# Decays of the first three blocks and their q and k, prepared on the chip instead of through DRAM and DMA transpositions

## The chip, the cores and the metric

The kernel runs on one core of one Trainium2 chip. The metric is the device time of one execution in microseconds, from the runtime's measurement around it. The engines are PE (TensorE, matmuls; its weight loads are PEld), DVE (VectorE), ACT (ScalarE), POOL (GpSimd) and SP (SyncE, which here only issues DMAs).

## The reference

Three stages follow each other over 4 batches (B) of 768 time steps (S). The first is a gated recurrence with 8 heads of 40, with a running maximum m that keeps the exponentials small:

```python
for t in range(S):
    m_new = np.maximum(f_gate[:, :, t] + m, i_gate[:, :, t])
    f_stab = np.exp(f_gate[:, :, t] + m - m_new)
    i_stab = np.exp(i_gate[:, :, t] - m_new)
    m = m_new
    C = f_stab[:, :, None, None] * C + i_stab[:, :, None, None] * np.einsum('bhd,bhe->bhde', vt, kt)
    n = f_stab[:, :, None] * n + i_stab[:, :, None] * kt
    h_tilde = np.einsum('bhde,bhe->bhd', C, qt)
    ...
    y[:, :, t] = o * h_tilde / np.maximum(np.abs(nq), 1.0)
```

The second is a gated MLP: relu(x @ w_in) is cut into u and v, v is normalised and mixed over time by w_spatial (768 x 768), and u times that goes through w_out. The third picks two of four experts for each step, and each expert is causal softmax attention with one head of 64. All inputs and the output are float32.

## The kernel before

**Tiling.** Time is cut into blocks of 128 steps, six to a batch, so there are 24 blocks n = (b, c). The recurrence is done a block at a time: inside a block as a matrix of decays times q-k products, between blocks through a state `cs`. Units of up to three blocks then go through the MLP, whose spatial mix needs whole batches, and through the attention. Float32 operands are mostly used as pairs of float16, a high part (a cast) and a low part (a subtraction), and a product is then three float16 matmuls. For the first NF = 6 blocks the product with v is done in float32 instead (vo,dd).

**The order.** The work is written as threads (generators) that yield the engine they want next and the buffers or signals they need. `ORDER` is a table of some thousands of thread names; `Flow.run` walks it and lets the named thread record its next piece. So the table alone sets in which order each engine's queue is filled. It was made by a planner that prices instructions with `_cost` (line 48), with DMAs and DMA transpositions among them. The strings of `CFG` say for each cast or subtraction which engine does it (a is ACT, v DVE, p POOL), and `on(what, x)` reads them. All instructions are recorded in one helper, so nearly all carry line L154, and the trace is read by the names of tiles.

**The head of the program.** `gates(j)` (line 576) loads the gates of half of the batches (j = 0: batches 0 and 1) into the tile aT, makes running sums (ff) and maxima (mm) by scans, and with two small matmuls carries the maxima over blocks. It then cuts the row of exponents into three bfloat16 parts, and `send` (648) writes each part with two DMAs to r_dram in DRAM. `ones` (654) fills the constant part of r_dram and clears the tile rows. `columns` (669) turns two gate rows into columns g_c and w_c. `m_load` (868) loads q and k (qkf), then v and the output gate (vo), and with a third DMA fetches six rows per head back from r_dram into rows. In `m_decay` (888) eight bfloat16 matmuls of these rows per block (four per PSUM bank g) give the exponents of the decay matrix, ACT takes the exponential of 128 x 512 at a time into dd, and POOL clears the part above the diagonal (affine_select). `mlstm` (1005) casts q and k into qs and transposes it with one DMA transposition per block (qkT<-qs, line 1028, issued on SP). `weights` multiplies q by k on PE, and DVE multiplies the product by dd (`dd<-g,dd`, called the first and second product of a block here). Then come the product with v (pn; vo,dd in float32), the part from the state (cs,qkT; none in a batch's first block), num, den, the output gate, a cast xs and its DMA transposition x1T<-xs, which feeds the MLP's first matmuls (wi,x1T).

**The loads of weights.** Beside this the weights w_in, w_spatial, wqkv, w_out come in through DMAs issued on ACT's queue. Float64 words are turned into float32 on DVE with three bit instructions (`u<-vn` and two `u<-vn,u`), then split into two float16 parts. They are most of what DVE does in the first 60 us besides the recurrence.

## Time and profile before

| | value |
|---|---|
| median of 3 runs | 523.35 us (520.78, 523.42, 523.35) |
| the profiled execution | 523.3 us, its span 521.6 us |
| PE busy in the span | 467.3 us (90%) |
| DVE | 435.6 us (84%) |
| ACT | 325.4 us (62%) |
| POOL | 272.2 us (52%) |
| granted TensorE clock, mean | 0.999 |

The span runs from the first instruction to the last; 1.7 us of the time lie around it. A busy share is a mean over a program whose head, middle and tail differ, so a table of stretches says more. Which of TensorE's two rates (1.2 or 2.4 GHz) holds is read from the duration of equal matmuls at two places. The float32 matmuls show as two records each: 16 records of vo,dd are eight matmuls.

### The profile page before, as it was taken

The page shows a single profiled execution, that of the slowest core. Times are in us where ns is not written, and L with a number is a line of the kernel's source. Part 1 is how long each engine was busy: PE and PEld are TensorE (multiplying, and loading weights), DVE is VectorE, ACT ScalarE, POOL GpSimd, SP SyncE. Part 2 cuts the span into 40 slices and gives each one's busy share as a digit, 9 for nine tenths or more (in the row PEclk, how much of TensorE's full clock was granted, in tenths as well). Part 3 has the DMA queues.
Part 4 walks back from the last instruction along what each step waited for, and adds up shares of the span by engine and source line. Part 5 has one row for each costly group of instructions (what it writes and reads, how often), then busy time and mean ns, then how long its engine had stood idle before and what let it go on. Part 6 is the DMA issues. An engine that isn't in the chain of part 4 may idle for free.

```text
span 521.6 us, 14133 instructions
## 1 busy us (share of the span) xinstructions
PE 467.3 (90%) x5288; PEld 336.5 (65%) x5288; DVE 435.6 (84%) x1133; ACT 325.4 (62%) x796; POOL 272.2 (52%) x437
## 2 busy tenths in 40 slices
...
GB/s 227 196 206 218 206 160 135 152 95 110 104 109 117 170 168 183 181 155 200 206 163 128 124 205 162 161 136 156 120 152 100 168 117 110 126 150 143 185 83 39
DMA packets 180443, 78.58 MB, mean 151 GB/s; under 512 B 160342, under 2 KB 169880, under 8 KB 180376
## 3 DMA queue, kind: packets, MB, share of 16 engines
...
## 4 chain that ended last, share of the span: by engine, by line
PE 54%; DVE 14%; DMA 13%; issue 6%; POOL 5%; ACT 4%; SPq 2%; ACTq 0%; POOLq 0%; DVEq 0%
PE g L154 51%; PE pst L154 3%; DMA x1T<-xs 3%; SPq L154 2%; DMA aT<-ahl 2%; POOL ahl L154 2%; DMA r_dram<-aT 2%; DMA rows<-r_dram 2%; DVE qs L154 2%; DMA qkst<-qkh 1%; DVE dd L154 1%; DVE vo L154 1%; ACT ee L154 1%; DVE u L154 1%; ACT aT L154 1%
## 5 line engine op out<-in xcount | busy, mean ns | idle before, releaser
L154 PE MATMUL g<-wsT,vn 128*128 128x384 f16 (+2 forms) x612 | 94.5, 307 | 0.0
L154 PEld LDWEIGHTS <-vn 128*128 128x128 f16 x648 | 59.3, 98 | 30.6
L154 POOL TENSOR_TENSOR ahl<-ee,ahl 128x128 f16<-128x128 f32 (+5 forms) x51 | 49.8, 981 | 29.4 <-DVE ahl L154 17.1
L154 POOL TENSOR_SCALAR_AFFINE_SELECT dd<-dd 128x512 f32<-128x512 f32 x48 | 36.4, 765 | 51.0 <-ACT dd L154 50.8
L154 PE MATMUL g<-wi,x1T 128*128 128x512 f16 x192 | 48.9, 400 | 4.8 <-DMA x1T<-xs 2.2
L154 ACT ACTIVATE ee<-g,sm 128x128 f32<-128x128 f32 (+3 forms) x64 | 33.4, 523 | 27.3 <-DVE sm L154 19.7
L154 PE MATMUL g<-gT,w_h 128*128 128x384 f16 (+2 forms) x288 | 47.6, 308 | 0.0
L154 PE MATMUL g<-x1T,wi 128*128 128x384 f16 (+2 forms) x288 | 46.4, 308 | 1.0 <-ACT u L154 0.5
L154 PEld LDWEIGHTS <-qkst 128*128 128x128 f16 x424 | 34.7, 98 | 18.2 <-issue 4.9
L154 DVE SCALAR_TENSOR_TENSOR dd<-g,dd 128x512 f32<-128x512 f32 x48 | 32.2, 680 | 13.8 <-PE g L154 8.3
L154 ACT ACTIVATE ee<-pst,sm 128x640 f32<-128x640 f32 (+1 forms) x32 | 27.1, 847 | 25.6 <-DVE sm L154 14.4
L154 ACT ACTIVATE vn<-vn,nt 128x512 bf16<-128x512 f32 (+1 forms) x48 | 36.3, 761 | 4.9 <-POOL nt L154 4.5
L154 DVE CUSTOM_DVE_ANT_0 g<-g,mask 128x128 f32<-128x128 f32 (+3 forms) x64 | 30.9, 502 | 7.7 <-PE g L154 7.6
L154 ACT ACTIVATE dd<-g 128x512 f32<-128x512 f32 x48 | 27.6, 593 | 15.5 <-PE g L154 15.3
L154 PE MATMUL g<-qkst 128*128 128x384 f16 (+4 forms) x224 | 34.9, 290 | 2.5 <-issue 2.3
L154 PEld LDWEIGHTS <-wi 128*128 128x128 f16 x288 | 26.2, 97 | 16.0 <-issue 2.8
L154 DVE CUSTOM_DVE_ANT_0 pst<-pst,mask 128x640 f32<-128x640 f32 (+1 forms) x32 | 28.5, 895 | 9.5 <-PE pst L154 9.0
L154 DVE TENSOR_TENSOR ahl<-ee,ahl 128x768 f16<-128x768 f32 (+5 forms) x45 | 33.5, 749 | 2.5 <-ACT ahl L154 1.8
L154 PEld LDWEIGHTS <-x1T 128*128 128x128 f16 x192 | 18.2, 100 | 26.1 <-issue 3.9
L154 PEld LDWEIGHTS <-w_h 128*128 128x128 f16 x288 | 26.4, 98 | 13.2
L154 PE MATMUL g<-vv,aT 128*128 128x64 f16 x1008 | 34.4, 193 | 0.4 <-ACT aT L154 0.4
L154 PEld LDWEIGHTS <-aT 128*128 128x128 f16 x1008 | 32.6, 98 | 1.9 <-ACT aT L154 0.5
...
## 6 DMA issues: line engine op xcount, KB each, us to landing
...
```

Of the source, the lines that this page charges most:

```text
L154: r = f(*args, **kw)
```

## The change

For the first three blocks (n < NE = 3) the decays come from a float32 copy f_e of the row ff: one float32 matmul per head spreads one row of f_e over 128 partitions, with a broadcast column of the identity as its stationary operand. The other half of the exponent is a column of i_c, which a new thread `first` makes with one PE transposition; it enters as the bias of the exponential, so that there are eight exponentials of 128 x 128 for a block instead of two of 128 x 512. These blocks fetch no rows from r_dram. For the same three blocks (n < NQ = 3) q and k are transposed by 16 PE transpositions into PSUM and two copies to qkT (thread `flip`), instead of the DMA transposition; qkf is given free after the copies. The planner's prices are raised for DMAs (250 in place of 290 bytes/ns) and DMA transpositions (210 in place of 180 ns per 128 columns). The whole table ORDER and all strings of CFG are new; two of them are shown.

```diff
@@ -50,11 +50,11 @@
-        return 1300.0 + 225.0 * max(0.0, n - 8.0), 1090.0 - 26.0 * n, (900.0, 180.0 * n + 40.0), False
+        return 1300.0 + 225.0 * max(0.0, n - 8.0), 1090.0 - 26.0 * n, (900.0, 210.0 * n + 40.0), False
-        return 335.0 if lane == "act" else 740.0 if across else 550.0, 1500.0 + o.nbytes() / 600.0, (600.0, 40.0 + max(60.0, o.nbytes() / 290.0)), False
+        return 335.0 if lane == "act" else 740.0 if across else 550.0, 1500.0 + o.nbytes() / 600.0, (600.0, 40.0 + max(60.0, o.nbytes() / 250.0)), False
@@ -319,175 +319,179 @@
...
 CFG = dict(
+    qt="aaaaaa",
+    fe="a",
+    ic="a",
...
-    Wl="------------vvvvvvvvvpvvvpvvpvvvvvvvvvvvvvvvvvpv",
...
-    vnl="ppvvvvvppvvvpvvvvpvpvvvv",
...
+    Wl="------------vvvvvvvvpvvvpvvpppvpvvvpvpvppvpvvpvv",
...
+    vnl="pppvvvpvvpvppvpvppvvpppv",
...
-TIM = dict(NF=6, NP=2, NX=21, last=(0, 1, 2, 3, 4, 5), units=((3, 3), (3, 3), (3, 3), (3, 2, 1)))
+TIM = dict(NQ=3, NE=3, NF=6, NP=2, NX=21, last=(0, 1, 2, 3, 4, 5), units=((3, 3), (3, 3), (3, 3), (3, 2, 1)))
 ORDER = """
-PX2 PX1 PO0 PW0 PW2 PO1 PW1 PO2 PG1 PO1 PG0 PL0 PX3 PI0 PG1 PW0 PX3 PG1 PS1 PG0 PG1 PG0 PG1 PL0 PO1 PG0 PM0 FS0 PG0
+PX2 PX1 PO1 PO0 PW2 PW1 PO2 PW0 PG1 PS1 PL0 PG0 PX3 PS4 PO1 PG1 PG1 PW1 PG1 PL0 PD0 PM0 PG1 FS0 PM0 PX3 PS1 PG1 FS1
...
@@ -562,6 +566,8 @@
     g_c = cp.tile([P, B, H, NC], F32, name="g_c")
     w_c = cp.tile([P, B, H, NC], F32, name="w_c")
     f_b = cp.tile([P, B, H, NC], F32, name="f_b")
+    f_e = cp.tile([96, P], F32, name="f_e")
+    i_c = cp.tile([P, 96], F32, name="i_c")
     r_dram = dr.tile([6, B, H, NC, 2, P], BF16, name="r_dram")
     wi = cp.tile([P, 2, 3, 1024], F16, name="wi")
     wi_h, wi_l = wi[:, 0], wi[:, 1]
@@ -593,6 +599,8 @@
         dve.tensor_tensor_scan(ff, ft, zt[:R], 0.0, op0=ALU.add, op1=ALU.add)
         dve.tensor_tensor(it, it, ff, op=ALU.subtract)
         dve.tensor_tensor_scan(mm, it, it, NEG, op0=ALU.max, op1=ALU.max)
+        if j == 0:
+            flow.fork(first(it), "FI", 0)
         mp, re = (row[0:1, x, 0:96].rearrange("p (g c) -> p g c", c=NC) for x in (3, 4))
         rfc = row[0:1, 5, 0:96]
         yield pe, "g"
@@ -616,13 +624,17 @@
         dve.tensor_copy(mc[:, 0:1], pc[:R, 128:129])
         dve.tensor_scalar(mc[:, 1:2], mm[:, P - 1:P], mc[:, 0:1], -1.0, op0=ALU.max, op1=ALU.mult)
         dve.tensor_scalar(ff, mm, mc[:, 0:1], None, op0=ALU.max)
+        if j == 0:
+            yield on("fe", 0)
+            on("fe", 0).cast(f_e, ff)
+            flow.signal("fe", 0)
         yield act
         act.activation(ft, ff, AF.Exp, bias=mc[:, 0:1], scale=-1.0)
         act.activation(mm, it, AF.Exp, bias=mc[:, 1:2])
         flow.signal("gw", j)
         flow.fork(columns(j, ft, mm), "FT", j)
         for x in range(3):
-            yield on("pc", 3 * j + x), *[("a", j, x - 2)] * (x > 1)
+            yield on("pc", 3 * j + x), *[("a", j, x - 2)] * (x > 1), *[("ic", 0)] * (j == 0 and x == 0)
             p = pcs[:, 2 * (x % 2):2 * (x % 2) + 2]
             on("pc", 3 * j + x).cast(p, am)
             flow.signal("pcs", j, x)
@@ -645,6 +657,17 @@
         yield dve, ("gc", 2 * j), *[("a", j, x) for x in range(3)]
         flow.done("aT", "aT")
 
+    def first(it):
+        R = 96
+        yield pe, "g"
+        pt = bank(R)
+        pe.transpose(pt, it, ident[:R, :R])
+        flow.signal("ip", 0)
+        yield on("ic", 0)
+        on("ic", 0).cast(i_c, pt)
+        flow.done("g")
+        flow.signal("ic", 0)
+
     def send(j, x, p):
         yield sp, ("pcs", j, x), ("rd", 0)
         for y in range(2):
@@ -878,7 +901,9 @@
         m["vf"], m["ex"] = (vo[:, x:y].rearrange("p (h d) -> p h d", h=H) for x, y in ((0, 328), (328, 648)))
         sp.dma_start(vo, qkvo[b, c, :, 640:1288])
         flow.signal("vo", n)
-        yield sp, "rw", seq("rw", n), ("rz", 0), *[("a", b // 2, x) for x in range(3)]
+        if n < TIM["NE"]:
+            return
+        yield sp, "rw", seq("rw", n - TIM["NE"]), ("rz", 0), *[("a", b // 2, x) for x in range(3)]
         m["own_rw"] = flow.take("rw")
         sp.dma_start(rows[0:6].rearrange("k h x s -> k h (x s)"), r_dram[:, b, :, c].rearrange("k h x s -> k h (x s)"))
         flow.signal("rw", n)
@@ -887,19 +912,29 @@
 
     def m_decay(n):
         b, c = divmod(n, NC)
-        yield pe, "dd", ("rw", n), seq("dd", n)
+        yield pe, "dd", ("qk" if n < TIM["NE"] else "rw", n), seq("dd", n)
         m = ml[n]
         m["dd"], m["own_dd"] = tile_("dd", [P, H, P]), flow.take("dd")
         dd = m["dd"]
 
         def half(g):
-            yield pe, "g", seq("de", 2 * n + g)
+            yield pe, "g", *[("fe", 0)] * (n < TIM["NE"]), seq("de", 2 * n + g)
             src = bank()
             for h in range(4):
-                pe.matmul(src[:, h * P:h * P + P], rows[:, 4 * g + h, 0], rows[:, 4 * g + h, 1], start=True, stop=True)
+                k = (4 * g + h) * NC + c
+                if n < TIM["NE"]:
+                    pe.matmul(src[:, h * P:h * P + P], ident[:96, k:k + 1].to_broadcast([96, P]), f_e, start=True, stop=True)
+                else:
+                    pe.matmul(src[:, h * P:h * P + P], rows[:, 4 * g + h, 0], rows[:, 4 * g + h, 1], start=True, stop=True)
             flow.signal("de", n, g)
-            yield act
-            act.activation(dd[:, 4 * g:4 * g + 4].rearrange("p h t -> p (h t)"), src, AF.Exp)
+            if n < TIM["NE"]:
+                yield act, ("ic", 0)
+                for h in range(4):
+                    k = (4 * g + h) * NC + c
+                    act.activation(dd[:, 4 * g + h], src[:, h * P:h * P + P], AF.Exp, bias=i_c[:, k:k + 1], scale=-1.0)
+            else:
+                yield act
+                act.activation(dd[:, 4 * g:4 * g + 4].rearrange("p h t -> p (h t)"), src, AF.Exp)
             flow.done("g")
             yield pool
             pool.affine_select(dd[:, 4 * g:4 * g + 4], dd[:, 4 * g:4 * g + 4], pattern=[[0, 4], [1, P]],
@@ -908,8 +943,9 @@
 
         for g in range(2):
             flow.fork(half(g), "FH", 2 * n + g)
-        yield pe, ("de", n, 0), ("de", n, 1)
-        flow.done(m["own_rw"])
+        if n >= TIM["NE"]:
+            yield pe, ("de", n, 0), ("de", n, 1)
+            flow.done(m["own_rw"])
 
     def m_out(n):
         yield act, ("vo", n)
@@ -1022,10 +1058,29 @@
 
         flow.fork(stack(1), "FS", 2 * n + 1)
         flow.fork(stack(0), "FS", 2 * n)
-        yield sp, "qkT", ("qs", n, 0), ("qs", n, 1), seq("qkT", n)
-        flow.done(m["own"])
-        qkT = tile_("qkT", [P, 16, P], F16)
-        sp.dma_start_transpose(out=qkT, in_=qs.rearrange("p a d -> p (a d)"))
+        if n < TIM["NQ"]:
+            yield pe, "qkT", seq("qkT", n)
+            qkT = tile_("qkT", [P, 16, P], F16)
+
+            def flip(x):
+                yield pe, "g", ("qs", n, x)
+                pt = bank().bitcast(F16).rearrange("p (k t) -> p k t", k=8)
+                for h in range(8):
+                    pe.transpose(pt[:120, h], qs[:, 8 - 8 * x + h, :120], ident_h)
+                yield on("qt", 2 * n + x)
+                on("qt", 2 * n + x).cast(qkT[:120, 8 - 8 * x:16 - 8 * x], pt[:120])
+                flow.done("g")
+                flow.signal("qt", n, x)
+
+            flow.fork(flip(1), "FX", 2 * n + 1)
+            flow.fork(flip(0), "FX", 2 * n)
+            yield pe, ("qt", n, 0), ("qt", n, 1)
+            flow.done(m["own"])
+        else:
+            yield sp, "qkT", ("qs", n, 0), ("qs", n, 1), seq("qkT", n)
+            flow.done(m["own"])
+            qkT = tile_("qkT", [P, 16, P], F16)
+            sp.dma_start_transpose(out=qkT, in_=qs.rearrange("p a d -> p (a d)"))
         flow.signal("qT", n)
         flow.fork(m_state(n), "FM", n)
         Ws = [None, None]
```

SP's queue at the start, before. rows and r_dram are the gate rows, qkf, vo the inputs of a block, qs and qkT its q and k:

```order
L154 DMA aT<-in_f_gate_dram 96x128 x2
L154 DMA qkf<-in_qkvo_dram 128x640
L154 DMA r_dram<-rows 576x1x128 x2
L154 DMA vo<-in_qkvo_dram 128x648
L154 DMA_TRANSPOSE qkT<-qs 128x16x128
L154 DMA r_dram<-aT 96x128 x2
L154 DMA qkf<-in_qkvo_dram 128x640
L154 DMA r_dram<-aT 96x128 x4
L154 DMA vo<-in_qkvo_dram 128x648
L154 DMA rows<-r_dram 6x8x256 x2
L154 DMA_TRANSPOSE qkT<-qs 128x16x128
```

And now:

```order
L154 DMA aT<-in_f_gate_dram 96x128
L154 DMA qkf<-in_qkvo_dram 128x640
L154 DMA aT<-in_f_gate_dram 96x128
L154 DMA vo<-in_qkvo_dram 128x648
L154 DMA r_dram<-rows 576x1x128 x2
L154 DMA qkf<-in_qkvo_dram 128x640
L154 DMA r_dram<-aT 96x128 x2
L154 DMA vo<-in_qkvo_dram 128x648
L154 DMA r_dram<-aT 96x128 x2
L154 DMA qkf<-in_qkvo_dram 128x640
L154 DMA qkst<-ee 64x256 x4
L154 DMA r_dram<-aT 96x128 x2
```

The transposition of block 0 stood before the sends of the gate rows; now the loads of three blocks and the sends come first, and the first rows<-r_dram and qkT<-qs stand some ten rows further down.

PE's queue at the start, before (the small matmuls on aT belong to the gates):

```order
L154 MATMUL g<-ident,aT 1x96 x4
L154 MATMUL g<-ones_83,aT 96x1 x2
L154 MATMUL g<-ident,aT 128x96 x4
L154 MATMUL g<-aT,ones_83 128x96
L154 LDWEIGHTS rows
L154 MATMUL g<-rows 128x128
```

And now, where ident_h,qs are the transpositions and f_e,ident the new decays:

```order
L154 MATMUL g<-ident,aT 1x96 x2
L154 MATMUL g<-ones_83,aT 96x1
L154 LDWEIGHTS qs
L154 MATMUL g<-ident_h,qs 120x128
...
L154 MATMUL g<-ones_83,aT 96x1
L154 MATMUL g<-ident,aT 128x96
L154 MATMUL g<-f_e,ident 128x128 x8
L154 MATMUL g<-ident,aT 128x96 x2
L154 MATMUL g<-f_e,ident 128x128 x4
```

Block 0's 16 transpositions stand between the small matmuls of the two halves of the gates, and its eight decays directly behind the second half's first ones, where the queue went on to the columns and then to the rows of r_dram.

DVE's queue around the first products, before (rows 46 to 53):

```order
L154 SCALAR_TENSOR_TENSOR qs<-qkf,qs 128x8x40
L154 TENSOR_SCALAR ee<-u 128x256
L154 SCALAR_TENSOR_TENSOR qkst<-vn,qkst 128x512
L154 COPY f_b<-g 128x96
L154 SCALAR_TENSOR_TENSOR dd<-g,dd 128x512 x2
L154 TENSOR_SCALAR u<-vn 128x256
L154 SCALAR_TENSOR_TENSOR u<-vn,u 128x256 x2
L154 SCALAR_TENSOR_TENSOR ee<-u,ee 128x256
```

And now (rows 50 to 58):

```order
L154 SCALAR_TENSOR_TENSOR qs<-qkf,qs 128x8x40
L154 SCALAR_TENSOR_TENSOR wi<-u,wi 128x256
L154 SCALAR_TENSOR_TENSOR ee<-u,ee 128x256
L154 SCALAR_TENSOR_TENSOR dd<-g,dd 128x512
L154 TENSOR_SCALAR u<-vn 128x256
L154 SCALAR_TENSOR_TENSOR u<-vn,u 128x256 x2
L154 SCALAR_TENSOR_TENSOR dd<-g,dd 128x512
```

The first product stands three rows further down the queue than before, and the two products of block 0 have a weight's three bit instructions between them.

## Rows read from the trace of the kernel before

**Rows 1.** Stretches of the span: length, then busy us (instructions) of each engine
```profile
core 0: us, PE busy (x) PEld busy (x) DVE busy (x) ACT busy (x) POOL busy (x), PEclk, DMA share, GB/s
0.00:35.00 35.00, 8.09 (x65) 5.88 (x66) 22.51 (x65) 13.23 (x36) 11.41 (x28) 1.00 0.81 200
35.00:65.00 30.00, 20.93 (x166) 16.74 (x164) 27.66 (x68) 15.83 (x38) 12.05 (x20) 1.00 0.89 223
65.00:105.00 40.00, 37.07 (x330) 24.45 (x329) 35.35 (x78) 28.73 (x66) 20.36 (x34) 1.00 0.66 146
105.00:521.60 416.60, 401.21 (x4733) 289.44 (x4730) 350.11 (x925) 267.58 (x658) 228.34 (x357) 1.00 0.72 142
```

**Rows 2.** Waits of PE, 0 to 70 us: us in total, times, longest
```profile
PE g L154 <- ACT aT L154: 11.7, 3, 9.0
PE g L154 <- DMA rows<-r_dram: 11.1, 3, 5.4
PE g L154 <- DVE aT L154: 7.8, 3, 4.1
```

**Rows 3.** Chain of waits, 0 to 60 us: start us, us, what
```profile
14.98 6.35 DMA r_dram<-aT
...
27.16 3.51 DMA rows<-r_dram
30.80 2.29 PE g L154 x36
...
44.31 3.16 SPq L154
...
58.38 5.93 DMA x1T<-xs
```

**Rows 4.** Timeline of DVE: start us, us, instruction, [idle before, what ended it]
```profile
20.23 0.29 DVE L154 TENSOR_SCALAR u<-vn 128x256 uint32<-128x256 uint32 x1 [2.33 <-DMA vn<-in_w_in_dram]
...
33.19 1.29 DVE L154 SCALAR_TENSOR_TENSOR dd<-g,dd 128x512 f32<-128x512 f32 x2 [4.93 <-PE g L154]
...
63.40 0.50 DVE L154 TENSOR_TENSOR num<-g,g_c 128x328 f32<-128x328 f32 x1 [1.76 <-PE g L154]
```

**Rows 5.** Tile qkT up to 75 us: SP's transpositions, min/median/max ns, first and last start
```profile
L154 SPq DMA_TRANSPOSE qkT<-qs x5: 1658/2177/3158, 11.2 to 65.4; - x5
```

**Rows 6.** The stretch up to the second product of block 6, columns as in Rows 1
```profile
0.00:104.60 104.60, 65.69 (x555) 46.88 (x556) 85.11 (x209) 57.43 (x138) 43.51 (x80) 1.00 0.77 187
```

**Rows 7.** Timeline of PE: start us, us of the group, instruction and records
```profile
24.66 0.74 PE L154 MATMUL g<-aT,ones 1*128 1x96 f32 x2 [8.99 <-ACT aT L154]
...
32.48 1.02 PE L154 MATMUL g<-qkT 120*128 120x128 f16 x8
...
35.12 3.58 PE L154 MATMUL g<-vo,dd 128*128 128x41 f32 x16
...
64.35 3.59 PE L154 MATMUL g<-wi,x1T 128*128 128x512 f16 x8 [0.99 <-DMA x1T<-xs]
...
85.07 1.88 PE L154 MATMUL g<-vo,dd 128*128 128x41 f32 x16
```

**Rows 8.** Groups by line and form, whole span: busy us, mean ns, idle before
```profile
L154 ACT ACTIVATE dd<-g 128x512 f32<-128x512 f32 x48 | 27.6, 593 | 15.5 <-PE g L154 15.3
L154 ACT ACTIVATE ee<-g,sm 128x128 f32<-128x128 f32 x16 | 5.8, 363 | 8.6 <-DVE sm L154 7.3 <-POOL ahl L154 1.0
L154 DVE TENSOR_TENSOR Wl<-dd,Wh 128x512 f16<-128x512 f32 x32 | 22.3, 700 | 1.1 <-POOL Wh L154 0.5 <-ACT Wh L154 0.5
L154 POOL TENSOR_TENSOR Wl<-dd,Wh 128x512 f16<-128x512 f32 x4 | 6.9, 1735 | 0.7 <-ACT Wh L154 0.7
L154 DVE TENSOR_TENSOR vn<-vn 128x512 f16<-128x512 f32 x17 | 12.6, 743 | 0.6 <-POOL vn L154 0.6
L154 POOL TENSOR_TENSOR vn<-vn 128x512 f16<-128x512 f32 x7 | 8.9, 1275 | 4.4 <-DVE vn L154 4.3
```

**Rows 9.** Waits of PE over the whole span, columns as in Rows 2
```profile
PE g L154 <- DMA x1T<-xs: 2.2, 4, 1.0
...
PE g L154 <- DMA oT<-os: 1.4, 1, 1.4
```

319 lines of the change are left out of this document (160 added, 159 removed).

## The prediction

> **What bounds the kernel now.** I read the table of stretches first, because a mean over 521.6 us hides where an engine is idle. PE is idle for 26.9 us of the first 35, for 9.1 of the next 30, for 2.9 of the next 40, and for 15.4 of the 416.6 that remain [rows 1]. From 105 us on PE works 96% of the time and is the bound there. Before 65 us it is starved, and the change is made there: whatever brings the head of the program to its end earlier is gained, if the rest keeps its shape.
>
> Then the waits of PE up to 70 us: 11.7 us for ACT on the gate tile aT, 11.1 for the DMA rows<-r_dram, 7.8 for DVE on aT [rows 2]. The chain of waits says which of them count. Its head goes through the DMAs that send the gate rows to DRAM, the DMA that fetches them, 2.29 us of PE and then DVE; later through a transposition's 3.16 us on SP and a fetch of x1T [rows 3]. This is the path that the change cuts.
>
> The third reading is DVE, which must not be left out: it is idle in only 19.5 of the first 104.6 us [rows 6], and between 33 and 62 us its timeline has no gap. From the first product on, DVE sets the pace of the head, with PE behind it. Its two waits that matter are 4.93 us for PE's first q-k product at 28 to 33 us, and 2.33 us for a load of w_in at 18 to 20 us [rows 4]. So the gain is bounded by what DVE gets back, not by PE's 26.9 us of idle time.
>
> **The parts, on DVE's clock.** I sum up to the second product of block 6 (dd, DVE; it ends at 104.6 us before), behind which both orders have the same pipeline.
>
> The first product. Before, it needs rows fetched from DRAM. After, block 0 needs only f_e and the transposed q and k, which PE makes itself. The cast of f_e stands behind the second gate scan, at about 14 us. Then come 8 f32 matmuls, 8 exps, and the mask on POOL. A price for the matmul with 128 columns in f32 is not in the trace. The nearest row is the f32 vo,dd at the low clock, 16 records that are 8 matmuls in 3.58 us, or 0.448 each. The low end is the same at the high clock, 1.88/8 = 0.235. The high end is 2 records (one f32 matmul of 96 columns) in 0.74 [rows 7]. I take 0.448, since PE is at the low clock here: 3.6 us for the eight. An exp of 128 columns takes 0.363 [rows 8], 8 of them 2.9 us. With the mask the inputs of the first product are there by about 23 us. In the new order DVE has about as much work ahead of its first product as before, row 53 against row 50, and reaches it at 33.2 - 4.9 - 2.3 = 26 us. So both waits can go: the whole 4.9, and 2.3 for the w_in load, which ran beside the first transposition (its issue starts at 11.2 and holds SP for some 3 us [rows 5]) that is now gone. Bounds: 4.9 goes unless f_e costs the high end (then 8 x 0.74 is 2.3 later, still in time); the 2.3 may stay whole. **-7.2 us** (bounds -4.9 and -7.2).
>
> What DVE takes on. At that second product of block 6 the new order has passed 201 rows of DVE against 190, with ten more instructions ahead (casts that ACT and POOL did, a relu, two vn subtractions). By the stretch's mean, 85.11/209 = 0.407 us [rows 6], ten cost 4.1; by the shorter forms that most of them have, some 3.0. **+3.0** (to +4.1). It is not work that can hide: DVE has no gaps there.
>
> PE's new work. It gets 24 f32 matmuls (24 x 0.448 = 10.8), 48 transpositions of 120 x 128 at the price of qkT x8, 1.02/8 = 0.128 [rows 7] (6.1), and loses 24 rows matmuls at about the same 0.128 (3.1): +13.8 us at the low clock. The 36.0 us of PE idle before 65 us cover it in sum, but not in place. Blocks 1 and 2 put 16 f32 matmuls (7.2 us) and 16 transpositions (2.0) between DVE's products, less 2.0 of rows matmuls. DVE then waits for the numerator of block 1 or 2. The nearest row is its wait of 1.76 us for num at 63.40 [rows 4]. A new wait of 0 to 4 us is possible, the upper end if half of the 7.2 us falls where DVE stands; I take **+1.0**, nearer that row than the end.
>
> ACT's new work is 24 exps for 6 (24 x 0.363 - 6 x 0.593 = 5.1 us) and six copies of 1024 columns, at most two exps of 512 columns each, so 7.1 us. ACT is idle for 21.8 us before 35 and for 14.2 before 65 [rows 1], so this is put at nothing. If ACT is late instead, the masked decay comes late, and that wait is already the +1.0.
>
> SP. Three transpositions leave the queue, of 1.66 to 3.16 us each [rows 5], and three fetches of rows. The sends of the gate rows (from 14.98 on) and x1T come forward. The sends no longer feed block 0, only block 3. The 3.16 us of SP and the fetch behind it in the chain [rows 3] are then not on DVE's path for block 2. But DVE had no wait there, so I count nothing more for it.
>
> Three spatial matmuls fewer stand ahead of the point on PE: **+0.5**. The longer stretch after it: DMA waits of PE, 2.2 for x1T and 1.4 for oT [rows 9]. The new plan prices DMAs higher and so starts them earlier; I take **-1.0** (0 to -3.6). PE's order elsewhere keeps its shape, so its other idle time is kept.
>
> Sum: -7.2 + 3.0 + 1.0 + 0.5 - 1.0 = -3.7. Against the profiled execution, 523.3 us (521.6 of span and 1.7 around it), that is **519.6 us**. The median of the three runs is 523.35, so no correction is needed; one of the three was 520.78.
>
> **The rivals.**
>
> A larger gain, 515.5 us. PE has dense f32 work from about 14 us on instead of gaps. Its clock could rise before 35 us, and not at 69 as now: the vo,dd matmuls take 3.58 us for 16 at 35 us and 1.88 at 85, and the first 512-column matmuls at 64 us still go at the low rate [rows 7]. At the high rate the new work costs 13.8 x 1.88/3.58 = 7.2 and the +1.0 vanishes. The old 20.93 us of PE work between 35 and 65 [rows 1] would shrink by up to 20.93 x (1 - 1.88/3.58) = 9.9, of which I let 3.1 reach the end, as DVE's work doesn't shrink: 519.6 - 1.0 - 3.1 = 515.5. Against it: the new matmuls still come in groups between waits. The Trainium skill, "TensorE: Matmul & The Clock Gate", section "Part 4: PE-mode transpose", says that the transpose mode doesn't count as PE work for the clock. By that rule the 48 transpositions lift nothing and only the f32 matmuls could. No row of before shows it, as the trace has no transpositions ahead of the rise. Chance 0.20.
>
> No change, 522.5 us. The decays of blocks 1 and 2 arrive late at 0.74 a matmul (7 us more on PE for 24), the num waits reach 3 to 4 us, and the load of w_in still holds DVE for 2.3: -4.9 + 3.0 + 3.5 + 0.5 - 1.0 = +1.1, or -1.2 with the 2.3 gone. So 522.1 to 524.4; I name 522.5, as the load's wait is the likelier to go. Here the change moves a wait rather than removes it. Chance 0.25.
>
> Slower, 527.5 us, one mechanism: the new strings put 12 of the Wl subtractions on POOL where 4 were, and 13 of the vn subtractions where 7 were. On POOL a Wl takes 1735 ns and on DVE 700, a vn 1275 and 743 [rows 8]. That is 8 x 1.035 + 6 x 0.532 = 11.5 us of added delay, strewn over the 416 us in which PE is 96% busy and can't catch up. It decides where POOL's result comes later than PE asks for it; where other PE work is ready in the meantime, nothing is lost. If two thirds of it, 7.7, reach PE, the time is 519.6 + 7.7 = 527.3. For it: POOL's queue also holds the masks, on which PE's products wait. Against: the same strings take other work off POOL, 431 instructions for 442 by the order, and in the stretch from 105 on it is busy for 228.34 of 416.6 us [rows 1], so that it has room. Chance 0.17.
>
> **How the numbers follow.** Forecast 0.38, larger gain 0.20, no change 0.25, slower 0.17. I regard 0.5%, 2.6 us, as what a measurement of this kernel can tell from no change, so the bounds are 520.7 and 525.9. The forecast itself reaches from 517 to 522.5 by the bounds above; about 0.31 of its 0.38 and all of the larger gain lie below 520.7. That gives 0.51 for faster, 0.32 for the same, 0.17 for slower. The range of 514.0 to 525.8 leaves out the slower case and a few in a hundred below.
>
> **What would show it.** In the new profile: DVE's first product dd at about 26 us with no wait for PE ahead of it (right), or a wait of over 2 us (the f32 price or the exps are wrong). The 24 f32 matmuls at 0.45 each, or 0.24 if PE is already fast. PE's wait for rows<-r_dram, 11.1 us, below 2. The second product of block 6 at about 101 us (104.6 now). New waits of DVE for num before 65 us: their sum against +1.0. Between 105 us and the end, PE's idle time of 15.4 us: 14 to 15 if I am right, above 19 in the slower case, with POOL's Wl or vn as what PE or DVE waited for. The forecast is wrong at its root if the point at block 6 comes forward by 3 us or more and the end doesn't, since I take the rest as shifted whole.

## The result, and the profile after

The changed kernel takes 525.03 us (median of 20 runs, 522.61 to 526.98), the kernel before 522.29 in as many runs beside it (519.85 to 524.98): a ratio of 1.0052, 95% interval [1.0035, 1.007]. It is slower by 2.7 us, where 3.7 us were forecast as a gain. The profiled execution took 525.3 us, its span 523.5; the one of before 523.3 and 521.6. Executions of one kernel differ by 4 to 5 us, so a difference of 1 us between two traces is not yet one between two kernels. The ratios, here and below, leave out as slow the runs that lie more than 1.5% above the shortest of their kernel; this matters most for h1, where they are the four longest of 12.

The table of stretches of the kernel after, as in [rows 1]:

```profile
core 0: us, PE busy (x) PEld busy (x) DVE busy (x) ACT busy (x) POOL busy (x), PEclk, DMA share, GB/s
0.00:35.00 35.00, 24.04 (x147) 21.22 (x148) 28.80 (x79) 22.29 (x60) 11.34 (x29) 1.00 0.69 209
35.00:65.00 30.00, 18.26 (x159) 13.93 (x158) 27.16 (x70) 16.89 (x43) 10.23 (x16) 0.89 0.81 183
65.00:105.00 40.00, 37.26 (x329) 24.51 (x326) 33.20 (x70) 24.90 (x57) 18.18 (x32) 0.91 0.53 125
105.00:523.50 418.50, 401.67 (x4730) 289.83 (x4730) 355.44 (x932) 268.50 (x659) 221.47 (x350) 1.00 0.71 141
```

PE is fuller by 16 us in the first stretch, and idle for longer in the second: 11.7 us against 9.1. Over the span its busy time rose from 467.3 to 481.2 us.

PE's waits up to 70 us, as in [rows 2]:

```profile
PE g L154 <- DVE aT L154: 7.1, 3, 4.1
PE g L154 <- DMA x1T<-xs: 6.0, 1, 6.0
PE g L154 <- DVE qs L154: 3.2, 3, 2.3
```

The 11.1 us for rows<-r_dram and the 11.7 for ACT on aT are gone (0.8 of the latter is left). New is a single wait of 6.0 us for x1T. The two timelines tell what became of the gain; first DVE's, as in [rows 4]:

```profile
25.91 0.68 DVE L154 SCALAR_TENSOR_TENSOR dd<-g,dd 128x512 f32<-128x512 f32 x1
...
33.08 0.20 DVE L154 RECIPROCAL den<-den 128x8 f32<-128x8 f32 x1 [1.13 <-POOL den L154]
...
45.55 0.50 DVE L154 TENSOR_TENSOR num<-g,g_c 128x328 f32<-128x328 f32 x1 [2.39 <-PE g L154]
...
70.25 0.69 DVE L154 SCALAR_TENSOR_TENSOR dd<-g,dd 128x512 f32<-128x512 f32 x1 [4.55 <-PE g L154]
```

The first product starts at 25.91 us without a wait, 7.3 earlier than in [rows 4]. At 70.25 us, in front of the first product of block 3, DVE stands for 4.55 us. The chain of waits says for what, as in [rows 3] (start us, us, what):

```profile
55.48 0.48 DVE xs L154 x2
56.39 6.69 DMA x1T<-xs
63.13 7.03 PE g L154 x28
70.25 0.69 DVE dd L154
```

The transposition of x1 of block 1 leaves SP at 56.39 and lands 6.69 us later. In [rows 3] it left at 58.38 and took 5.93. Behind it PE needs 7 us, with the group of wi,x1T first, before block 3's product can run. PE's timeline there, and at 80 to 87 us, as in [rows 7]:

```profile
26.64 2.07 PE L154 MATMUL g<-f_e,ident 96*128 96x128 f32 x8 [0.21 <-DVE dd L154]
...
40.53 3.58 PE L154 MATMUL g<-vo,dd 128*128 128x41 f32 x16
...
54.71 2.04 PE L154 MATMUL g<-vo,dd 128*128 128x41 f32 x16
63.13 3.60 PE L154 MATMUL g<-wi,x1T 128*128 128x512 f16 x8 [5.98 <-DMA x1T<-xs]
...
82.14 0.38 PE L154 MATMUL g<-qkT 120*128 120x128 f16 x4 [0.52 <-DVE w_l L154]
83.34 1.98 PE L154 MATMUL g<-vo,dd 128*128 128x41 f32 x16 [0.81 <-DVE dd L154]
85.95 0.68 PE L154 MATMUL g<-cs,qkT 80*128 80x41 f16 x15 [0.60 <-DVE cs L154]
86.46 3.21 PE L154 MATMUL g<-wi,x1T 128*128 128x512 f16 x8
```

The same eight matmuls wi,x1T, 1.89 us at the high clock, take 3.60 at 63 us and 3.21 at 86. Short stretches with the granted clock (the column behind the engines) show why:

```profile
54.00:58.00 4.00, 3.15 (x35) 2.62 (x33) 3.93 (x11) 3.02 (x7) 2.47 (x4) 1.00 0.87 183
58.00:62.00 4.00, 0.00 (x0) 0.00 (x0) 3.93 (x12) 2.39 (x7) 1.96 (x5) 0.56 1.09 271
62.00:66.00 4.00, 2.87 (x7) 1.04 (x8) 3.66 (x13) 0.00 (x0) 0.00 (x0) 0.50 0.96 198
66.00:70.00 4.00, 4.00 (x23) 2.22 (x22) 0.00 (x0) 2.78 (x8) 1.28 (x2) 0.66 0.72 179
70.00:82.00 12.00, 11.46 (x117) 8.02 (x115) 11.47 (x28) 7.26 (x18) 4.08 (x8) 1.00 0.40 94
82.00:86.00 4.00, 2.44 (x23) 2.18 (x23) 4.00 (x7) 3.23 (x9) 3.54 (x6) 0.97 0.57 132
86.00:90.00 4.00, 4.00 (x43) 2.06 (x43) 3.61 (x10) 0.92 (x3) 0.00 (x0) 0.60 0.25 49
```

The column reads 1.00 also where the trace holds no record of the clock, as it does ahead of 55 us; there the matmuls tell it, the sixteen vo,dd that take 3.58 us at 40.53 and 2.04 at 54.71. So the clock rose at about 55 us already (2.4 GHz). It fell to 1.2 GHz while PE waited for x1T with nothing to do, and once more behind three waits of 0.5 to 0.8 us at 82 to 86 us. DMA is nearly full while x1T is under way.

Last the stretch to the second product of block 6, cut at the first product as [rows 6] can be:

```profile
0.00:25.90 25.90, 15.15 (x102) 12.66 (x103) 21.13 (x61) 16.51 (x46) 9.49 (x25) 1.00 0.76 228
25.90:105.10 79.20, 64.41 (x531) 46.99 (x529) 68.12 (x158) 47.66 (x114) 30.36 (x52) 0.91 0.64 151
```

The same two pieces of before:

```profile
0.00:33.20 33.20, 7.08 (x58) 5.14 (x58) 20.74 (x62) 12.42 (x33) 10.57 (x27) 1.00 0.79 197
33.20:104.60 71.40, 58.61 (x500) 41.73 (x499) 64.37 (x148) 45.01 (x106) 32.93 (x54) 1.00 0.77 182
```

The first piece is 7.3 us shorter, the second 7.8 longer: DVE is busy for 3.75 us more in it and idle for 4.05 more (11.08 against 7.03). So block 6 ends at 105.1 us, against 104.6.

### The profile page after: what moved, and what is told of

Its sections match the earlier page's. It is cut to its first block, busy times and chain, and to the rows that moved or that the text cites. A ratio compares the mean times of both kernels' runs of the same rounds, so it can differ in the third digit from the quotient of the medians.

```text
span 523.5 us, 14278 instructions
## 1 busy us (share of the span) xinstructions
PE 481.2 (92%) x5361; PEld 349.5 (67%) x5361; DVE 444.6 (85%) x1149; ACT 332.6 (64%) x817; POOL 261.2 (50%) x426
## 4 chain that ended last, share of the span: by engine, by line
PE 64%; DVE 22%; DMA 6%; issue 4%; ACT 2%; POOL 1%; SPq 0%; ACTq 0%; DVEq 0%; POOLq 0%
PE g L154 61%; DMA x1T<-xs 3%; PE pst L154 3%; DVE ahl L154 2%; DVE dd L154 2%; DVE u L154 2%; DVE qs L154 2%; DMA oT<-os 2%; DVE vo L154 1%; DVE xs L154 1%; DVE wsT L154 1%; DVE pst L154 1%; DMA qkf<-in_qkvo_dram 1%; DVE aT L154 1%; POOL ahl L154 1%
## 5 line engine op out<-in xcount | busy, mean ns | idle before, releaser
L154 POOL TENSOR_SCALAR_AFFINE_SELECT dd<-dd 128x512 f32<-128x512 f32 x48 | 34.3, 723 | 57.2 <-ACT dd L154 56.9
L154 PE MATMUL g<-wi,x1T 128*128 128x512 f16 x192 | 50.2, 408 | 8.3 <-DMA x1T<-xs 7.1
L154 POOL TENSOR_TENSOR ahl<-ee,ahl 128x384 f16<-128x384 f32 (+5 forms) x39 | 38.7, 995 | 21.2 <-ACT ahl L154 11.2
L154 DVE TENSOR_TENSOR ahl<-ee,ahl 128x768 f16<-128x768 f32 (+5 forms) x57 | 39.9, 707 | 2.4 <-ACT ahl L154 1.9
L154 DVE CUSTOM_DVE_ANT_0 g<-g,mask 128x128 f32<-128x128 f32 (+3 forms) x64 | 31.1, 499 | 7.2 <-PE g L154 6.0
L154 PE MATMUL g<-qkst 128*128 128x384 f16 (+4 forms) x224 | 36.0, 291 | 0.8 <-issue 0.5
L154 PE MATMUL g<-vv,aT 128*128 128x64 f16 x1008 | 34.3, 193 | 0.8 <-ACT ee L154 0.7
L154 ACT ACTIVATE dd<-g 128x512 f32<-128x512 f32 x42 | 24.1, 595 | 15.6 <-PE g L154 15.3
```

The costliest lines, as they stand in the source:

```text
L154: r = f(*args, **kw)
```

## The experiments

"Blocks" in the table are the ends of DVE's second product of blocks 0, 3, 6 and 8 in the profiled execution, in us. Each ratio is to the kernel before on the same chip.

| kernel | median us | ratio [95%] | block 0 | 3 | 6 | 8 |
|---|---|---|---|---|---|---|
| before | 522.29 | 1 | 34.5 | 73.4 | 104.6 | 124.0 |
| after | 525.03 | 1.0052 [1.0035, 1.007] | 28.3 | 72.3 | 105.1 | 126.0 |
| c0, after again | 525.2 | 1.0069 [1.004, 1.0098] | 28.1 | 70.0 | 104.1 | 126.3 |
| g3, turns by DMA | 525.35 | 1.0054 [1.003, 1.0078] | 29.2 | 71.4 | 106.2 | 128.6 |
| e2, flips late | 525.18 | 1.0071 [1.0042, 1.01] | 28.0 | 72.4 | 106.0 | 126.8 |
| e3, less on DVE | 525.43 | 1.0079 [1.0056, 1.0101] | 29.0 | 71.2 | 104.7 | 126.8 |
| f6, x1T first | 529.79 | 1.0129 [1.0082, 1.0175] | 28.0 | 73.6 | 107.2 | 129.5 |
| f2, fill at x1T | 524.5 | 1.0032 [0.9998, 1.0066] | 28.3 | 71.7 | 104.8 | 125.5 |
| g1, fill late | 523.44 | 1.0020 [0.9996, 1.0044] | 28.1 | 70.5 | 102.8 | 123.6 |
| e4, POOL back | 523.67 | 1.0042 [1.0015, 1.007] | 27.9 | 71.3 | 103.5 | 124.3 |
| i2, g1 and e4 | 522.82 | 1.0024 [0.9993, 1.0055] | 28.4 | 71.7 | 103.4 | 124.2 |
| f3, before with banks | 522.1 | 0.9999 [0.9965, 1.0034] | 33.8 | 74.4 | 105.6 | 124.8 |
| h1, before with fill | 521.63 | 0.9964 [0.9932, 0.9996] | 31.2 | 70.0 | 101.2 | 120.4 |
| e1, old order | 526.08 | 1.0081 [1.0047, 1.0116] | 34.3 | 73.5 | 104.9 | 125.4 |
| g4, old order, late | 523.05 | 1.0021 [0.9999, 1.0043] | 30.9 | 69.6 | 100.7 | 123.5 |
| i1, g4 with fill | 523.05 | 1.0022 [0.9992, 1.0051] | 31.1 | 71.1 | 102.3 | 123.5 |
| i3, i1 with more fill | 521.31 | 0.9987 [0.9961, 1.0012] | 30.9 | 68.3 | 100.1 | 120.8 |

The start of the program scatters as well. Up to 40 us the kernel before, f3 and h1 run the same instructions on every engine (f3 with other PSUM banks), and their block 0 stands at 34.5, 33.8 and 31.2 us. Eight profiles share the changed kernel's start (after, c0, e2, e4, f2, f6, g1, i2), and there it is 27.9 to 28.4. So the early start is clear of the scatter, but its size of 6.2 us holds for this one profile of before.

### The order kept, the work on chip: e1, g4, and banks: f3

The ORDER of before with the decays and turns of blocks 0 to 2 on chip; e1 has block 0's part ahead of the gate scans' later steps:

```diff
-TIM = dict(NF=6, ...
+TIM = dict(NQ=3, NE=3, NF=6, ...
 ORDER: ... PW1 PG0
+PG0 FI0 FI0 PD0 FH0 FH1 FH0 FH1 FH0 FH1 PM0 FX1 FX0 FX1 FX0
 PM0 PX3 ...
```

> The order and engine split of the kernel before, with only the on-chip part of the change put in: decays of blocks 0 to 2 from f_e and i_c, their q and k by transpositions on PE, and block 0's decays moved forward in the order. If the new order and split are what lost the time (DVE got 4.2 us more work and new waits of 4.0 us up to the second product of block 6), the on-chip part alone keeps most of the 6 us by which the second product of block 0 comes forward, and the time is 517 to 519, 4 us under the kernel before. If the on-chip part itself loses it, because PE's 13 us of added work delays what DVE waits for next, the time is 522 or more, no better than before.

Measured 1.0081. The first product came no earlier. DVE's longest wait ahead of it:

```profile
DVE aT L154 <- ACT aT L154: 7.7, 1, 7.7
```

Block 0's exps and copies stood in front of the gate's own exps in ACT's queue, and DVE waited for these. That says what the place was worth, not the decays; g4 puts them behind:

```diff
 ORDER: ... PS5 FT1
+PD0 FH0 PM0 FX1 FX0 FH1 FH0 FX1 FX0 FH1 PM0 PL1 FH0 FH1
 PG0 PS1 ...
```

> As e1_old_order (order and engine split of the kernel before, decays, q and k of blocks 0 to 2 on chip), but block 0's exponentials and copies stand behind the gates' work on ACT, not ahead of it: in e1 they held DVE for 7.65 us, and its first product was no earlier than before. Now the first product should come at 26 to 28 us (33.2 before). If that wait was worth what the prediction took, some 5 us, the time is 517 to 519. If what follows is set by other things (arrival of x1T, loads, PE at its low rate), the lead is gone by block 3 and the time is 521 to 524.

The time is 1.0021 [0.9999, 1.0043]. Now the lead is there in the profile: 3.6 us at block 0, 3.8 at block 3, 3.9 at block 6, and 0.5 at block 8. PE's row at the point where it is lost, and the stretch around it (columns as in the first table):

```profile
111.81 2.85 PE L154 MATMUL g<-wi,x1T 128*128 128x512 f16 x8 [2.01 <-DMA x1T<-xs]
```

```profile
112.00:116.00 4.00, 4.00 (x13) 1.66 (x12) 1.56 (x5) 1.40 (x5) 0.00 (x0) 0.58 0.90 167
```

Behind a wait of 2.01 us for x1T the clock is at its low level. The kernel before has no such wait there. Before reading g4 and e1 against before, one more difference had to be priced: the rebuilt order lands in other PSUM banks. f3 is before with the banks of e1 and nothing else:

```diff
+BANKS = """PG1:0,2,0,2,0,2 PG0:1,3,1,3,1,3 FH0:101,101,101 ...
```

> The kernel before, instruction for instruction in its order, with only the choice of PSUM banks (tile g) as it fell out in e1_old_order: 235 of 377 threads get other banks. e1 was 4 us slower, though the second product of its block 6 came only 0.3 us later and its order from there on is that of the kernel before. If the banks are what it lost behind the head, this kernel is 2 to 4 us slower than the kernel before too. If not, it is within 1 us of it.

0.9999 [0.9965, 1.0034]: the banks make no difference that could be measured.

### Which half: g3, e2

g3 keeps the new order and the decays on PE, but turns q and k of blocks 0 to 2 by DMA:

```diff
-TIM = dict(NQ=3, NE=3, ...
+TIM = dict(NQ=0, NE=3, ...
```

> The changed kernel with half of the change undone: q and k of blocks 0 to 2 are transposed by DMA again (at the place where PE's transpositions began), the decays stay on PE. If PE's 48 transpositions, their six copies on ACT and their places ahead of other work cost more than the DMA transpositions did, the time falls by 1 to 3. If the DMA transpositions hold SP and the DMA engines, as the change has it, the sends, loads and x1T behind them come later, and the time rises by 2 to 5.

e2 lets PE do block 2's transpositions later:

```diff
 ORDER: ... FS5 FU3
-FX4
 PO0 FM0 PS2
-FX5 ...
 PM0 PM1
+FX5 FX4 FX5 FX4
 PS5 FH4 ...
```

> The changed kernel, with block 2's transpositions on PE moved behind block 1's product with v in PE's queue. In the changed kernel they stand ahead of it, wait 2.28 us for DVE's qs, take 1.96 us, and DVE then waits 2.39 us for num of block 1. If this place in the queue is what cost, that wait falls below 0.5 and the time by about 2, to 523. If the head is set by the transfer of x1T (PE waits 5.98 us for it) or by DVE's amount of work, the wait moves elsewhere and the time stays at 525.

1.0054 and 1.0071: neither the transpositions nor their place make a loss or a gain that could be measured. In g3 the first product is as early as in after, again without a wait, so the early start comes from the decays on chip:

```profile
26.76 0.68 DVE L154 SCALAR_TENSOR_TENSOR dd<-g,dd 128x512 f32<-128x512 f32 x1
```

In e2 the wait for num of block 1, which was to fall below 0.5 us, is still there:

```profile
44.98 0.50 DVE L154 TENSOR_TENSOR num<-g,g_c 128x328 f32<-128x328 f32 x1 [2.48 <-PE g L154]
```

### What DVE carries: e3

```diff
-    rz="v", ... x1h="aavvapvaaaapaaapaapaaaaa",
+    rz="p", ... x1h="aaaaapvaaaapaaapaapaaaaa",
```

and likewise in gt, wh, ch, ru and pc: ten small operations of the head go from DVE to ACT and POOL.

> The changed kernel, with ten entries of the head's engine split put back from DVE to ACT or POOL as in the kernel before (casts of cs for blocks 0 and 3, wx 4, xs 2 and 3, two gate columns, one gate part, two relus u, the clearing of rows): 4.2 us less of DVE work before the second product of block 6. If DVE's work sets the pace of the head, that product comes forward by 2 to 4 us and the time is 521.5 to 523. If waits set it (x1T, clock), DVE only idles more and the time stays within 1 us of 525.

The stretch to 105.1 us, where the kernel after has DVE busy for 89.25 us:

```profile
0.00:105.10 105.10, 81.44 (x633) 61.42 (x633) 86.93 (x208) 67.57 (x170) 41.37 (x78) 0.84 0.69 170
```

DVE has 2.3 us less to do and block 6 ends at 104.7 instead of 105.1; the time is 1.0079. What is taken from DVE comes back as idle time, and the kernel is no faster. That DVE's amount of work doesn't set the end of the head is likely but not shown: in this profile the clock was also low for longer (PEclk 0.66 at 82 to 92 us, 0.83 in after).

### The wait for x1T: f6, f2

f6 puts the transposition qkT of block 3 and the load qkf of block 4 behind x1T of block 1 on SP (the place from which PL4 goes is in a stretch left out here):

```diff
 ORDER: ... PI1 PI3
-PM3
 PR0 PM1 ... PI0 PM1
+PM3 PL4
 PO0 PN0 ...
```

> The changed kernel, with the transposition of block 3's q and k and the load of block 4's issued behind the second x1T's transposition on SP, and not 4.9 and 3.0 us ahead of it. If x1T lands late (6.69 us after its issue) because it queues behind those 0.85 MB, it lands 2 to 3 us earlier, PE's wait of 5.98 falls to 3 to 4, and the time falls by 1 to 2.5, if nothing else takes the place. If the head is bound elsewhere, by the loads of weights or by DVE, the time stays at 525, or rises by 1 because block 3's q and k now come late.

PE's row for x1T, to be set beside 63.13 [5.98] above:

```profile
60.59 3.59 PE L154 MATMUL g<-wi,x1T 128*128 128x512 f16 x8 [3.77 <-DMA x1T<-xs]
```

x1T is there 2.5 us earlier, and yet block 3 comes 1.3 later (73.6) and the time rises to 1.0129. PE's q-k products of block 3 are not late: they start at 68.3 and 69.4 us, 69.8 and 70.9 in after. DVE is, because ahead of them in its queue stands its part of block 4's q and k, which waits for ACT's cast of the load that was moved too:

```profile
64.86 1.46 DVE L154 SCALAR_TENSOR_TENSOR qs<-qkf,qs 128x320 f16<-128x320 f32 x2 [5.67 <-ACT qs L154]
```

So one transfer that is moved forward makes another late. What an earlier x1T alone would give, this run doesn't tell.

f2 keeps the order and fills the wait with 22 products of the identity with itself, which nobody reads:

```diff
+        for _ in range(TIM["fill"]):
+            pe.matmul(pt, ident_h, ident_h..., start=True, stop=True)
 ORDER: ... FS9 PM2
+PF0
 PN1 PL3 ...
```

> The changed kernel, with 22 extra matmuls of 512 columns on PE (identity times identity, read by nobody) where PE waits 5.98 us for the second x1T; they take 22 x 0.236 = 5.2 us if PE is at the high rate there. If the fall of the clock that follows this wait (low from 58.5 to 68.7 us) is what gives block 3 its late product, the matmuls behind the wait run at the high rate (3.60 us for the eight of wi,x1T becomes 1.9), the first product of block 3 comes 2.5 us earlier and the time falls by 2 to 3, to 522.5. If the clock isn't what holds the head, the time stays at 525; if the filler itself runs at the low rate it takes 9.9 us and the time is 528 or more.

```profile
63.64 2.51 PE L154 MATMUL g<-wi,x1T 128*128 128x512 f16 x8 [2.05 <-DMA x1T<-xs]
```

Of the wait 2.05 us are left, and the clock holds until 64.8 us and then falls for 3.4. The eight matmuls take 2.51 instead of 3.60 us, and block 3 comes 0.6 earlier, not 2.5, which is less than two profiles of after differ by (72.3 and 70.0). The time is 1.0032 [0.9998, 1.0066], not told apart from after.

### The clock behind 80 us: c0, g1, h1

c0 is the kernel after, unchanged, with another execution profiled.

> The changed kernel once more, as it is, for comparison with the others of this group on the same chip, and for a second profile of it. All theories: 1.004 to 1.007 of the kernel before, near 525; the second product of block 6 on DVE between 104 and 106 us, as in the first profile (105.1).

It measures 1.0069, with block 6 at 104.1. But the lead is lost at other places than in the first profile: block 3 is at 70.0, 3.4 us ahead of before, behind a shorter wait, and the clock is low from 82.0 to 88.8 and from 105.9 to 109.3 us.

```profile
67.96 0.69 DVE L154 SCALAR_TENSOR_TENSOR dd<-g,dd 128x512 f32<-128x512 f32 x1 [2.43 <-PE g L154]
```

g1 puts 14 such products into four short waits of PE between 80 and 106 us:

```diff
+TIM = dict(fill=(2, 3, 3, 6,), NQ=3, ...
 ORDER: ... FW8
+PF0
 FW9 PK4
+PF1
 PM4 ... FS12
+PF2
 PM4 ... FR6
+PF3
 PM6 ...
```

> The changed kernel, with 14 extra matmuls of 512 columns (read by nobody) in PE's queue at four places where PE waited between 82 and 106 us: 2 ahead of block 4's second q-k products, 3 ahead of its product with v, 3 ahead of its product with the state, 6 ahead of block 6's product with v; 0.24 us each at the high rate, no longer than the waits. In seven profiles with the new order the clock fell once or twice more after 80 us (low for 3.4, 6.8 or 10.2 us in all up to block 8), in those with the old order never, and blocks 3 to 8 took about 0.4 us more for each low us. If these falls come from the waits, the clock stays high from 70 us on, the second product of block 8 comes 1.4 to 3 us sooner and the time falls by 1.5 to 2.5, to 523 (1.002 of before). If the falls don't come from these waits or cost nothing, the time stays at 1.005 to 1.007.

The stretch that holds the first of them (columns as in the first table), and the same of after:

```profile
82.00:92.00 10.00, 9.41 (x103) 6.73 (x102) 8.65 (x19) 5.81 (x16) 4.61 (x9) 1.00 0.67 135
```

```profile
82.00:92.00 10.00, 8.44 (x85) 5.68 (x85) 8.50 (x18) 6.01 (x17) 4.33 (x8) 0.83 0.55 112
```

The clock stays high, and the time is 1.0020 [0.9996, 1.0044] against 1.0052 and 1.0069 for the two measurements of after: unread work on PE makes the kernel some 2 us faster. The difference is just beyond what the intervals allow, which overlap at their edges. The traces go with it: of the ten profiles with the new order, the eight without these products show one to three falls of the clock between 75 and 113 us, the two with them (g1 and i2) none. The same in the kernel before, with 16 products at 42 to 60 us, where its clock was low until 70:

```diff
+TIM = dict(fill=(10, 2, 4,), NF=6, ...
 ORDER: ... PD2 PI2
+PF0
 FH4 ... PI1
+PF1
 PM2 ... FS9
+PF2
 PN1 ...
```

> The kernel before, with 16 extra matmuls of 512 columns (read by nobody) in three waits of PE: 10 at 45 to 50 us ahead of block 2's decays, 2 ahead of its product with v, 4 ahead of the second x1T. If PE's low rate up to 70 us holds the head, PE is at the high rate from about 50 us on, the 16 matmuls on x1T take 3.8 instead of 7.3 us, block 3's product comes 2 to 3 us sooner and the time falls by 1 to 3, below both kernels. If the head is set by DVE and the DMAs, block 3 comes as before and the time stays within 1 us of the kernel before.

0.9964 [0.9932, 0.9996], block 6 at 101.2. It is the fastest of all by its ratio, but that doesn't show that the products made it so. Its 12 runs scatter from 515.01 to 526.32, and the medians of all runs are 521.63 and 522.08, a ratio of 0.9991. In the profile 3.3 of the 3.4 us by which block 6 comes earlier are there at block 0 already (31.2 against 34.5), and the first of the products starts at 42.0 us. Nor did the clock stay high from 50 us on: it is low at 48.5 to 55.3 and 58.7 to 65.6.

### POOL's strings: e4, i2

```diff
-    Wl="------------vvvvvvvvpvvvpvvpppvpvvvpvpvppvpvvpvv",
+    Wl="------------vvvvvvvvvpvvvpvvpvvvvvvvvvvvvvvvvvpv",
-    vnl="pppvvvpvvpvppvpvppvvpppv",
+    vnl="ppvvvvvppvvvpvvvvpvpvvvv",
```

> The changed kernel, with the two strings of the slower rival put back as before: 4 instead of 12 Wl subtractions and 7 instead of 13 vn subtractions on POOL, the others on DVE. If POOL's slower subtractions cost what the part behind block 6 lost (418.4 us for 417.0 in the two profiles), the time falls by 1.5 to 3. If not, it stays at 525, or rises by up to 3 since DVE takes some 10 us of work.

1.0042 [1.0015, 1.007], between before and after and not clearly apart from after. i2 has this and the fillers of g1:

> The changed kernel with the 14 fillers of g1_fill_late (results never read) and POOL's and DVE's shares of Wl and vn as in the kernel before (e4_pool_back). Theory that the two losses are separate and add: about 1 us under g1, 521 to 522.5 us, ratio 0.997 to 1.001, block 8 about 1 us earlier than in g1 (123.58). Rival, that e4 gained because its clock fell less or later, so that nothing is left to gain once the clock stays high: the same as g1, ratio 1.001 to 1.004.

1.0024 [0.9993, 1.0055], the same as g1 alone. With the clock kept up nothing is left for POOL's strings to lose that could be measured.

### The lead that holds or doesn't: i1, i3

i1 is g4 with eight products in its wait of 2.01 us:

```diff
+TIM = dict(fill=(8,), NQ=3, ...
 ORDER: ... FW15 FW14
+PF0
 PN6 ...
```

> The kernel of g4_old_order_late with eight products of the identity with itself (128x512, their results are never read) put into PE's 2.01 us wait for x1T at 109.8 us, in front of the matmuls that in g4 ran at 111.81. Theory (the lead of a shortened start is lost where PE's clock falls behind a wait): the clock stays at its high level through 112 to 116, the second product of block 8 stands about 3.5 us before that of the kernel before instead of 0.5, and the time is about 3 us under g4's, some 519 to 520 us, ratio 0.994 to 0.997. Rival (the lead is lost at block 8 whatever the clock does, because block 8's inputs come late): the clock stays high and block 8 still stands within 1 us of the kernel before, ratio 1.000 to 1.003. A second rival (the lead arrives at block 8 but is given back in the rest of the span): block 8 at -3.5 and ratio 1.000.

```profile
111.73 1.89 PE L154 MATMUL g<-ident_h 128*128 128x512 f16 x8
113.46 1.89 PE L154 MATMUL g<-wi,x1T 128*128 128x512 f16 x8
```

```profile
112.00:116.00 4.00, 4.00 (x21) 1.90 (x20) 3.43 (x7) 2.68 (x7) 1.04 (x2) 1.00 0.40 79
```

The clock stays high, wi,x1T needs 1.89 us instead of 2.85, and nothing is won: 1.0022 against 1.0021, block 8 at 123.5 in both. My theory for this run said 0.994 to 0.997 and fell. Two things are to be seen in the traces. The fillers hold PE for 1.73 us, and in this execution x1T may have been there before they ended, so that they give back part of what the clock brings. And the lead was smaller from the start: at block 3 2.3 us, where g4, with the same instructions up to there, had 3.8; g4's clock rose at 51.2 us and i1's at 56.0. One execution is that uncertain.

i3 has twelve more in the wait for dd at 54 us and three ahead of x1T at 61:

```diff
-TIM = dict(fill=(8,), ...
+TIM = dict(fill=(12, 3, 8,), ...
 ORDER: ... FM1 PN0
+PF0
 PM1 ... PN0 FS9
+PF1
 PN1 ...
```

> The kernel of i1 with fifteen more fillers (results never read): twelve in PE's 3.3 us wait for dd at 54 us and three in front of the products that wait for x1T at 61 us. Theory: in g4 the clock was at its low level from about 58 to 65; held high there, the work of blocks 2 and 3 runs faster and block 3 comes another 1 us earlier: some 518 to 519.5 us, ratio 0.992 to 0.996. Rival (at these places DVE and the transpositions set the pace and PE only follows): block 3 stands as in i1, and the times agree within 0.5 us.

```profile
60.00:80.00 20.00, 16.41 (x158) 10.31 (x155) 18.82 (x44) 14.04 (x32) 8.90 (x16) 1.00 0.82 179
```

Here the clock is high from 55.6 us on without a fall, block 3 comes 5.0 us before that of the kernel before, block 8 3.2, and the span ends 5.2 earlier (516.4). Whether a lead that gets past block 8 is kept can't be read from such pairs: in h1 3.5 us at block 8 are 1.6 at the end, and from block 8 to the end the profiles take between 394.5 and 399.6 us. The profiled execution was the shortest of the twelve (518.51); their median is 521.31 and the ratio 0.9987 [0.9961, 1.0012], short of the 0.992 to 0.996 of my theory and not clearly apart from i1.

## Why the prediction was wrong, point by point

**The first product: right.** -7.2 us were forecast, from two waits of DVE that would both go. The product starts at 25.91 us, 26 was said, and both waits are gone: -7.3. But the reason given for the 2.3 of w_in, that the first DMA transposition is gone, is not borne out: in g3 that transposition is back, it holds SP for 3.5 us from 8.9 on, and DVE doesn't wait for w_in either; nor does it in h1, which has the old order. That part of the number was luck. The f32 matmul costs 2.07/4 = 0.52 us in the group at 26.64 (two records each), 0.448 was taken. All 24 take 11.9 us and the 48 transpositions 6.4, 10.8 and 6.1 in the forecast; that PE's busy time rose by 481.2 - 467.3 = 13.9 us, as the 13.8 of the forecast, is in part luck too.

**What DVE takes on: mis-sized.** +3.0 were set down, up to 4.1. DVE's busy time to block 6 rose from 85.11 [rows 6] to 89.25 us, by 4.1. That is the bound and not the value. In e3 a lighter DVE left the end where it was, so this isn't likely to be what decides.

**New waits: too small, and at the wrong place.** +1.0 was set down for the numerators of blocks 1 and 2; behind the first product DVE's idle time grew by 4.05 us. The numerators are a small part of it: block 1's waits 2.39 us now and block 2's waited 1.76 before, +0.6. Block 0's den waits 1.13 for POOL. The largest wait stands at block 3, 4.55 us for PE, where before DVE waited 1.81:

```profile
72.10 1.29 DVE L154 SCALAR_TENSOR_TENSOR dd<-g,dd 128x512 f32<-128x512 f32 x2 [1.81 <-POOL nt L154]
```

This is the step that failed. I summed on DVE's clock and wrote of SP and x1T "DVE had no wait there, so I count nothing more for it". A lead of DVE is worth something only up to the next point at which another chain arrives. Here it is xs, the transposition, its landing, and 7 us of PE, most of it at 1.2 GHz, and it came forward by just 1.2 us (63.13 against 64.35 in [rows 7]): SP sent it 2.0 earlier, and it took 0.8 longer beside the loads of weights. The lead of 6.2 us at block 0 is 4.1 at block 2 and 1.1 at block 3. DVE does 2.8 us more work between the second products of these two (12.6 against 9.8) and still stands for 4.55 at the end of it, so its work doesn't set that end. The group with this chain was quoted [rows 3] and costed as a thing that SP does, not as the next thing that is late.

The other profiles bear this out. In 15 of all 17 the second product of block 3 ends 7.6 to 9.5 us after PE starts on this x1T (9.0 before, 9.2 after); the two others are f6, where DVE waits for ACT, and i3, whose clock was high (6.3). Of the 15, DVE doesn't wait there at all in g3, and in before, g4, h1 and i1 it waits for POOL and not for PE. And PE starts on it at 61.8 to 65.5 us with the old order and at 60.6 to 63.7 with the new one: the change moves it by little. That is read from traces; the one run that moved x1T, f6, moved a load with it. How much is lost here differs: in c0 the lead is still 3.4 at block 3, and the rest goes behind it.

**The three spatial matmuls** were 0.5 and are not seen apart from the rest.

**"The rest keeps its shape": wrong.** The prediction called itself wrong at its root if block 6 came forward by 3 us or more and the end didn't; in the changed kernel block 6 didn't come forward at all, but in g4 it did, by 3.9, and the span ended at 521.7 us, where before has 521.6. From block 3 to block 8 before takes 50.6 us and after 53.7. Part of it is the clock. Before, it is high from 70 us on to the end of the work; after, it falls once more behind the waits at 82 to 86 us, and in c0 twice, for some 10 us in all, where that stretch took 56.3 us. g1 and i2 without the fall measure 1.0020 and 1.0024 against 1.0052 and 1.0069: some 2 us, by two kernels of which each alone is at the edge of its interval. Part is not the clock: with none of it g1 and i2 still take 53.0 and 52.4. All ten profiles of the new order have a wait at block 7 for POOL, of 1.4 us (2.1 to 2.9 in c0, f6 and g3):

```profile
114.70 1.29 DVE L154 SCALAR_TENSOR_TENSOR dd<-g,dd 128x512 f32<-128x512 f32 x2 [1.44 <-POOL dd L154]
```

The decays of block 7 (rows matmuls, exp on ACT, mask on POOL) stand 7.2 us behind block 6 on PE's queue there (112.29 against 105.1) and 5.7 in the kernel before (110.31 against 104.6), with 18 spatial matmuls between them and the last vx,Wl where before has 9. What this costs is open: no run moved it, and DVE's whole idle time between the second products of blocks 6 and 7 is 2.1 us against 1.7 before, between those of blocks 7 and 8 1.6 against 0.1.

**DMA waits of PE: nothing.** -1.0 was set down. In the kernel after:

```profile
PE g L154 <- DMA x1T<-xs: 7.1, 3, 6.0
...
PE g L154 <- DMA oT<-os: 2.4, 2, 1.8
```

Without the 6.0 that is 1.1 + 2.4 = 3.5 us against 3.6 in [rows 9].

The measured sum: -7.3 at the first product, +7.8 to block 6 (3.75 of work on DVE and 4.05 of waits), +1.5 to block 8, nothing behind it (397.5 us to the end, 397.6 before). That is +2.0, as the profiled executions differ by (525.3 and 523.3); the medians differ by 2.7.

**The rivals.** The larger gain had part of the right event and the wrong sign. The clock did rise early, at 55 us and not at 70, if not before 35 as it said, and the rise bought little because the next wait took it away; that the clock can fall again, and at waits of under 1 us, was in no case of mine. In e4, which runs the same instructions up to there, it even was high from 16.6 to 20.0 us and low again until 54.2, and block 0 stood at 27.9 instead of 28.3. On the rule of the Trainium skill that the prediction named there ("TensorE: Matmul & The Clock Gate", "Part 4: PE-mode transpose"), the runs say nothing: PE had no long stretch of transpositions alone. The case of no change named late decays and num waits, and 522.1 to 524.4; the mechanism was that in small part (+0.6 at the numerators), though the idea that a wait moves instead of going is what happened. The slower case named POOL: its Wl take 1213 ns and not 1735, PE's idle time behind 105 us is 16.8 us (15.4 before, over 19 was the mark), and in e4 and i2 nothing comes back that could be measured:

```profile
L154 POOL TENSOR_TENSOR vn<-vn 128x512 f16<-128x512 f32 x13 | 17.1, 1318 | 1.3 <-DVE vn L154 0.9 <-ACT vn L154 0.4
L154 POOL TENSOR_TENSOR Wl<-dd,Wh 128x512 f16<-128x512 f32 x12 | 14.6, 1213 | 11.4 <-ACT Wh L154 10.4 <-DVE Wh L154 1.0
```

**What stays open.** With the clock held up the new order comes out at 1.002, not at the forecast 0.993, and the rest is put together from traces: x1T at block 3 and the decays of block 7. That x1T sets block 3 and what the decays of block 7 cost is therefore argued from traces and not shown by a run that moves either alone. The old order with the same work on chip has the forecast lead, 3.9 us at block 6, in one execution (g4), 2.3 in another (i1) and 4.5 in a third (i3), and none of the three kernels can be told from the kernel before. So decays and transpositions on chip without the new order gained nothing that could be measured (g4, 1.0021 [0.9999, 1.0043]); i3, at 0.9987, has 23 unread products with them.
